# A first transform whose result is turned by DMA transposes in SBUF instead of a bounce through DRAM

## The chip, the cores and the metric

One core of one Trainium2 chip runs the kernel. The metric is the device time of one execution in microseconds (us); a kernel's time is the median of its runs. On one core a run counts as slow when it is over 1.5% above the fastest of the same kernel.

## The reference, cut to what matters

Two stages over x of 8 batches x 3072 tokens x 256 channels:

```python
X = np.fft.rfft(x, axis=1)                       # along the 3072 tokens
Yr = Xr @ w_r - Xi @ w_i + b_r                   # complex 256 x 256 product, soft shrink by 0.01
Yi = Xr @ w_i + Xi @ w_r + b_i
y = np.fft.irfft(Y, n=3072, axis=1)
# then, on y:
xk, xr = mu_k * y + (1 - mu_k) * y_prev, mu_r * y + (1 - mu_r) * y_prev
k = np.maximum(xk @ w_k, 0.0)                    # 256 -> 1024
out = sigmoid(xr @ w_r) * (k * k @ w_v)          # 1024 -> 256
```

## The kernel before: the parts that the change touches

The transform of 3072 = 96 x 32 points is made in two matmul stages. The first (96 points, matrix FT) is followed by a change of layout, the second (32 points, with twiddles, G) needs its rows by group. Then come the complex product (`mix`), the second transform's inverse (`back`, GI), a second change of layout through DRAM (Vdr, the "second bounce"), and the inverse of the first (`last`, FI). Tokens follow, six tiles of 512 per batch.

A Python scheduler with modelled durations decides the order in which each engine gets its instructions. `done[...]` holds the moment at which it assumes something to be there. The order is fixed when the program is built.

```python
    def first(b, t0, t1):                # batches 2 to 7: bounce through DRAM
        ...
                for i in range(2):
                    nc.tensor.matmul(ps[:96, 512 * i:512 * i + 512], FT,
                                     xt[:, 4 * p + 2 * i:4 * p + 2 * i + 2, :], start=True, stop=True)
        ...
                def store(k):
                    nc.sync.dma_start(out=Adr[b][:, 8 * q:8 * q + 8, :], in_=a)
        ...
                def fetch(k):
                    for hf in range(2):
                        A2[b, hf] = a2_pool.tile([128, NG // 2, D], BF16, name="A2")
                        for cj in range(4):
                            r0 = 24 * cj + 12 * hf
                            nc.sync.dma_start(out=A2[b, hf][32 * cj:32 * cj + 32],
                                              in_=Adr[b][r0:r0 + 12].rearrange("g n d -> n g d"))

    def direct(b, t0, t1, t2):           # batches 0 and 1: channels as rows, then turned on TensorE
        ...
                for i in range(8):
                    nc.tensor.matmul(pv[:, i, :], xt[:, i, 128 * c:128 * c + 128], FT, start=True, stop=True)
        ...
                    if c == 1 and b == 1:
                        load_x(2, q)     # x of batch 2
        ...
        def turn(u):                     # 8 identity matmuls and one copy out of PSUM, six times
        ...
    # in back(), after the last piece of V is in SBUF:
                def store(k):
                    for cj in range(4):
                        nc.sync.dma_start(out=Vdr[b][...], in_=vt[32 * cj:32 * cj + 32])
                    if u == NU - 1:
                        at(k + (3.0 if b == 0 else WRITE_US), fetch)      # WRITE_US = 5.0
                def fetch(k):
                    for q in (2, 3, 0, 1):
                        nc.sync.dma_start(out=V2[b, q], in_=Vdr[b][:, 8 * q:8 * q + 8, :])
                    done["V2", b] = k + READ_US                           # READ_US = 7.0
```

All of these DMAs, and the output stores, are issued by SP in one order (SP's lines below, from 198.89 us in the change, show it).

## Time and profile before

| | before |
|---|---|
| median, 4 runs beside the changed kernel | 617.68 us |
| span of the profiled run | 615.4 us |
| first W_k matmul (tokens begin) | 74.8 us |
| PE busy, mean granted clock | 571.8 us (93%), 0.987 |
| period of the steady part, start to start of one W_v group | 70.3 us, once 74.9 |

PE is TensorE, PEld its weight loads, DVE VectorE, ACT ScalarE, SP the engine that issues DMAs; "PE L609" is the matmul of line 609. The changed kernel's line numbers differ: W_k is L609 before and L560 after, W_v L653 and L604, the last transform L523 and L474, the second transform L381/L398 and L326/L343, the first transform in channels-as-rows form L335 and L279. In the versions made for the experiments the numbers shift again. The lines of the page and the trace stand in the prediction, with their readings. "The head" is the time until the tokens begin, "the steady part" the rest. In the lines, out<-in names what a transfer or an instruction writes and reads: Vdr<-V is a store of V, V<-Vdr its fetch, A<-X a transpose, xs<-in_x_dram a load of x. A line of a timeline begins with its start and its length in us. A "hole" is a time in which PE waits.

### The profile page before, as it was taken

The page shows a single profiled execution, that of the slowest core. Times are in us where ns is not written, and L with a number is a line of the kernel's source. Part 1 is how long each engine was busy: PE and PEld are TensorE (multiplying, and loading weights), DVE is VectorE, ACT ScalarE, POOL GpSimd, SP SyncE. Part 2 cuts the span into 40 slices and gives each one's busy share as a digit, 9 for nine tenths or more (in the row PEclk, how much of TensorE's full clock was granted, in tenths as well). Part 3 has the DMA queues.
Part 4 walks back from the last instruction along what each step waited for, and adds up shares of the span by engine and source line. Part 5 has one row for each costly group of instructions (what it writes and reads, how often), then busy time and mean ns, then how long its engine had stood idle before and what let it go on. Part 6 is the DMA issues. An engine that isn't in the chain of part 4 may idle for free.

```text
span 615.4 us, 12311 instructions
## 1 busy us (share of the span) xinstructions
PE 571.8 (93%) x4823; PEld 431.9 (70%) x4891; DVE 517.6 (84%) x839; ACT 436.0 (71%) x476; POOL 23.3 (4%) x52
## 2 busy tenths in 40 slices
PE   4775899999999999979999999999999999999995
PEld 3764666667777777657776778677776778777664
DVE  6774699878998999959988888979888889989883
ACT  6764596776877677757787768876787777667662
POOL 7001000000000000000000000000000000000000
PEclk9999799999999999989999999999999999999999
DMA  8948237982668755695568946686347833462223
GB/s 150 175 82 181 65 62 166 242 185 55 133 142 236 172 110 132 144 231 118 108 136 200 195 114 129 141 236 147 83 98 189 190 93 87 87 172 65 70 64 78
DMA packets 68686, 84.06 MB, mean 137 GB/s; under 512 B 8978, under 2 KB 53780, under 8 KB 68628
## 3 DMA queue, kind: packets, MB, share of 16 engines
q1 hardware_dynamic: 62916, 69.24, 45.4%
q0 software_dynamic: 5712, 14.03, 14.7%
q8 instruction: 38, 0.62, 0.4%
q14 instruction: 20, 0.16, 0.1%
HBM read 50.07 MB, written 47.19 MB: 158 GB/s over the span
## 4 chain that ended last, share of the span: by engine, by line
PE 79%; DMA 8%; DVE 5%; ACT 5%; issue 2%; SPq 1%; POOL 0%; ACTq 0%; POOLq 0%; DVEq 0%
PE banks L653 25%; PE banks L609 24%; PE banks L426 11%; PE banks L636 6%; DMA V<-Vdr 4%; DMA Vdr<-V 3%; PE banks L523 3%; PE banks L398 3%; PE banks L452 3%; PE banks L280 3%; ACT rl L615 2%; DMA xs<-in_x_dram 1%; DVE Y L442 1%; DVE z L440 1%; DVE V L229 1%
## 5 line engine op out<-in xcount | busy, mean ns | idle before, releaser
L615 ACT ACTIVATE rl<-banks 128x1024 bf16<-128x1024 f32 x192 | 195.4, 1033 | 76.1 <-PE banks L609 75.0
L609 PE MATMUL banks<-xk,wk 128*128 128x512 bf16 x700 | 190.1, 379 | 5.1 <-ACT A L227 0.8
L653 PE MATMUL banks<-wv,k 128*128 128x256 bf16 x1536 | 183.4, 273 | 0.3 <-DVE k L621 0.3
L653 PEld LDWEIGHTS <-k 128*128 128x128 bf16 x1536 | 149.6, 98 | 30.3 <-issue 1.2
L621 DVE TENSOR_TENSOR k<-rl 128x1024 bf16<-128x1024 bf16 x192 | 131.0, 685 | 16.8 <-ACT rl L615 16.1
L609 PEld LDWEIGHTS <-wk 128*128 128x128 bf16 x768 | 73.0, 97 | 59.5 <-issue 3.2
L426 PEld LDWEIGHTS <-XT 128*128 128x128 bf16 x768 | 74.4, 98 | 16.1 <-issue 0.6
L426 PE MATMUL banks<-wr,XT 128*128 128x256 bf16 x384 | 73.5, 273 | 0.2 <-ACT XT L227 0.2
L426 PE MATMUL banks<-wi,XT 128*128 128x256 bf16 x384 | 73.5, 273 | 0.0
L587 DVE SCALAR_TENSOR_TENSOR xk<-diff,muk,YT 128x512 bf16<-128x512 bf16 x96 | 70.0, 745 | 0.5
L587 DVE SCALAR_TENSOR_TENSOR xr<-diff,mur,YT 128x512 bf16<-128x512 bf16 x96 | 68.9, 745 | 0.0
L227 ACT ACTIVATE YT<-banks 128x768 bf16<-128x768 f32 x60 | 46.3, 814 | 30.0 <-PE banks L523 28.1
L660 DVE TENSOR_TENSOR o<-banks,rg 128x1024 f32<-128x1024 f32 x48 | 58.5, 1219 | 6.6 <-PE banks L653 6.6
L227 ACT ACTIVATE z<-banks 128x1024 bf16<-128x1024 f32 x39 | 39.9, 1024 | 23.7 <-PE banks L426 23.7
L227 ACT ACTIVATE XT<-banks 128x1024 bf16<-128x1024 f32 (+2 forms) x45 | 44.4, 989 | 14.3 <-PE banks L398 14.3
L636 PE MATMUL banks<-wrm,xr 128*128 128x256 bf16 x384 | 50.6, 275 | 1.8 <-ACT rl L615 1.7
L641 ACT ACTIVATE rg<-banks 128x1024 bf16<-128x1024 f32 x48 | 49.5, 1031 | 0.9 <-PE banks L636 0.9
L227 ACT ACTIVATE A<-banks 96x1024 bf16<-96x1024 f32 (+1 forms) x43 | 43.4, 1015 | 8.0 <-PE banks L280 6.7
L636 PEld LDWEIGHTS <-xr 128*128 128x128 bf16 x384 | 37.4, 98 | 12.7 <-issue 2.6
L523 PE MATMUL banks<-FI,V 96*128 96x96 f16 x512 | 33.5, 216 | 12.9 <-DMA V<-Vdr 12.6
L227 ACT ACTIVATE V<-banks 128x1024 bf16<-128x1024 f32 x35 | 36.0, 1028 | 13.2 <-PE banks L452 11.1
L523 PEld LDWEIGHTS <-V 96*128 96x128 bf16 x512 | 29.5, 104 | 20.6 <-DMA V<-Vdr 14.7
(98 smaller groups left out, 447.3 us busy)
## 6 DMA issues: line engine op xcount, KB each, us to landing
out_dram<-o SPq DMA_DIRECT2D x192, 128.0 KB, 2.3
xs<-in_x_dram POOLq DMA_DIRECT2D x32, 384.0 KB, 6.2
Vdr<-V SPq DMA_DIRECT2D x192, 64.0 KB, 1.8
V<-Vdr SPq DMA_DIRECT2D x32, 384.0 KB, 6.8
Adr<-A SPq DMA_DIRECT2D x24, 384.0 KB, 5.5
A<-Adr SPq DMA_DIRECT2D x48, 192.0 KB, 5.6
wk<-in_moe_w_k_dram POOLq DMA_DIRECT2D x1, 512.0 KB, 11.6
wv<-in_moe_w_v_dram POOLq DMA_DIRECT2D x1, 512.0 KB, 13.9
```

Of the source, the lines that this page charges most:

```text
L227: nc.scalar.activation(out, in_, AF.Copy, bias=0.0, scale=1.0)
L280: nc.tensor.matmul(ps[:96, 512 * i:512 * i + 512], FT, xt[:, 4 * p + 2 * i:4 * p + 2 * i + 2, :], start=True, stop=True)
L426: nc.tensor.matmul(o, lhs, w[:, c, :], start=(w is wr and c == 0), stop=(w is wi and c == NCD - 1))
L523: nc.tensor.matmul(pv[:, c, :, i, :], V2[b, n2 // 8][:, n2 % 8, 128 * c:128 * c + 128], FI, start=True, stop=True)
L587: nc.vector.scalar_tensor_tensor(out=m[:, c, :], in0=df[:, c, :], scalar=mu[:, c:c + 1], in1=yp[:, c, :], op0=ALU.mult, op1=ALU.add)
L609: nc.tensor.matmul(ps[:, 512 * f:512 * f + 512], wk[:, c, 128 * ff:128 * ff + 128], xk[:, c, :], start=(c == 0), stop=(c == NCD - 1))
L615: nc.scalar.activation(rl, ps, AF.Relu, bias=0.0, scale=1.0)
L621: nc.vector.tensor_tensor(out=k2, in0=rl, in1=rl, op=ALU.mult)
L636: nc.tensor.matmul(ps[:, 256 * q:256 * q + 256], xr[:, c, 128 * q:128 * q + 128], wrm[:, c, :], start=(c == 0), stop=(c == NCD - 1))
L641: nc.scalar.activation(rg, ps, AF.Sigmoid, bias=0.0, scale=1.0)
L653: nc.tensor.matmul(ps[:, 256 * q:256 * q + 256], K2[t][:, ff, 128 * q:128 * q + 128], wv[:, ff, :], start=(ff == 0), stop=(ff == NCF - 1))
L660: nc.vector.tensor_tensor(out=o.rearrange("p q d -> p (q d)"), in0=ps, in1=rg, op=ALU.mult)
```

## The change

Its intent: take the first bounce (3 MB through DRAM a batch) away from the DMA engines, make the first transform cheaper on TensorE, and free TensorE and the copy engines of the turning in batches 0 and 1. All batches now use the channels-as-rows form, and eight DMA transposes turn it inside SBUF. With it come a split of the two sine activations that make table G, the x loads of batch 2 moved behind the arrival of V of batch 0, a scheduler period of 70.5 instead of 71.5, and the last token tile in two parts.

```diff
+    PARTS = 4
     def first(b, t0, t1):
-        (16 matmuls 96x512 a batch, store to Adr by quarter, fetch by group)
+                for i in range(8):
+                    nc.tensor.matmul(pv[:, i, :], xt[:, i, 128 * c:128 * c + 128], FT, start=True, stop=True)
+                ...
+                def turn(k):
+                    n = NG // PARTS
+                    for i in range(PARTS):
+                        hf, g0 = n * i // 12, n * i % 12
+                        if g0 == 0:
+                            A2[b, hf] = a2_pool.tile([128, NG // 2, D], BF16, name="A2")
+                        for cc in range(NCD):
+                            nc.sync.dma_start_transpose(
+                                out=A2[b, hf][:, g0:g0 + n, 128 * cc:128 * cc + 128],
+                                in_=X1[b, cc][:, n * i:n * i + n].rearrange("p g r n -> p (g r n)"))
+                        for u in range(NU):
+                            if n * i < 4 * u + 4 <= n * i + n:
+                                done["A2", b, u] = k + 2.5 + 10.0 * (i + 1) / PARTS
-    def direct(b, t0, t1, t2):           (the PE turn of batches 0 and 1)
...
                     done["V2", b] = k + READ_US
+                    if b == 0:
+                        nc.gpsimd.tensor_copy(out=n1c[0:96], in_=V2[0, 1][:, 0, 0:1])
+                        for q in range(4):
+                            load_x(2, q)
...                                       (v_unit: the last tile in two halves, on the queues of SP and ACT)
-    P = 71.5
+    P = 70.5
```

The `tensor_copy` on GpSimd only makes that queue wait: it reads V2 and so holds the loads behind it. This hold is called "the gate" below.

More of the change, by code (lines that the diff above doesn't have):

```diff
@@ L55, in pool @@
         return ctx.enter_context(tc.tile_pool(name=name, bufs=bufs))
-    a_pool, a2_pool, xt_pool, xt0_pool = pool("ap", 3), pool("a2p", 4), pool("xtp", 3), pool("xt0p", 1)
+    x1_pool, a2_pool, xt_pool, xt0_pool = pool("x1p", 2), pool("a2p", 4), pool("xtp", 3), pool("xt0p", 1)
     r1_pool, ym_pool, v_pool, v2_pool = pool("r1p", 2), pool("ymp", 3), pool("vp", 3), pool("v2p", 4)
@@ L173, in make_g @@
     def make_g():
-        for j, sc in ((0, sc0), (1, sc1)):
-            nc.scalar.activation(G[:, :, :, j, :], ang, AF.Sin, bias=0.0, scale=sc)
+        nc.scalar.activation(G[:, :, :, 1, :], ang, AF.Sin, bias=0.0, scale=sc1)
         nc.vector.tensor_scalar(out=G0[:, 0], in0=G[:, 0, 1], scalar1=-1.0, scalar2=None, op0=ALU.mult)
@@ L262, in ready @@
             return None if f is None else max(r, f)
-    Adr, A2, Vdr, V2, YT = {}, {}, {}, {}, {}
+    X1, A2, Vdr, V2, YT = {}, {}, {}, {}, {}
     READ_US, WRITE_US = 7.0, 5.0
+    NU = NG // 4
+    PARTS = 4
     def first(b, t0, t1):
-        live = {}
-        def make(q, p):
-            def issue(ps, h, end):
-                if p == 0:
-                    if q == 0:
-                        Adr[b] = dram.tile([2 * 48, N2, D], BF16, name="Adr")
-                    live["A"] = a_pool.tile([96, 8, D], BF16, name="A")
-                xt, a = xs[b, q], live["A"]
-                for i in range(2):
-                    nc.tensor.matmul(ps[:96, 512 * i:512 * i + 512], FT,
-                                     xt[:, 4 * p + 2 * i:4 * p + 2 * i + 2, :], start=True, stop=True)
-                def evac(k):
-                    e = copy(k, a[:, 4 * p:4 * p + 4, :], ps[:96].rearrange("p (n d) -> p n d", n=4),
-                             1.03, 1.22)
-                    release(h, e)
-                    if p == 1:
-                        at(e, store)
-                def store(k):
-                    nc.sync.dma_start(out=Adr[b][:, 8 * q:8 * q + 8, :], in_=a)
-                    done["a", b, q] = k + WRITE_US
-                    n = 4 * b + q + 4
-                    if 8 <= n < 4 * B:
-                        load_x(n // 4, n % 4)
-                        done["x", n // 4, n % 4] = k + 9.0
-                    if q == 3:
-                        at(k + WRITE_US, fetch)
-                def fetch(k):
-                    for hf in range(2):
-                        A2[b, hf] = a2_pool.tile([128, NG // 2, D], BF16, name="A2")
-                        for cj in range(4):
-                            r0 = 24 * cj + 12 * hf
-                            nc.sync.dma_start(out=A2[b, hf][32 * cj:32 * cj + 32],
-                                              in_=Adr[b][r0:r0 + 12].rearrange("g n d -> n g d"))
-                        for u in range(3 * hf, 3 * hf + 3):
-                            done["A2", b, u] = k + READ_US * (1 + hf) / 2
-                at(end, evac)
-            needs = [("x", b, q), "FT"] + [("K", 0)] * (b == 2)
-            if q == 3 and p == 1 and b >= 2:
-                needs.append(("mid", b - 2))
-            if q == 0 and p == 0 and b >= 2:
-                needs.append(("A2", b - 2, NU - 1))
-            n = 4 * b + q - 3
-            if p == 0 and n >= 8:
-                needs.append(("a", n // 4, n % 4))
-            return Unit(t0 + (t1 - t0) * (2 * q + p) / 8, 0.44, needs, issue)
-        return [make(q, p) for q in range(4) for p in range(2)]
@@ L324, in direct @@
-    def direct(b, t0, t1, t2):
-        live = {}
         def make(q, c):
             def issue(ps, h, end):
-                if q == 0 and c == 0:
-                    live["X1"] = yt_pool.tile([128, NCD, NG, 4, 32], BF16, name="YT")
-                x1, xt = live["X1"], xs[b, q]
+                if q == 0:
+                    X1[b, c] = x1_pool.tile([128, NG, 4, 32], BF16, name="X1")
+                x1, xt = X1[b, c], xs[b, q]
                 pv = ps.rearrange("p (n f) -> p n f", n=8)[:, :, 0:96]
@@ L337, in evac @@
                 def evac(k):
-                    e = copy(k, x1[:, c, :, :, 8 * q:8 * q + 8], pv.rearrange("p n (r g) -> p g r n", r=4),
+                    e = copy(k, x1[:, :, :, 8 * q:8 * q + 8], pv.rearrange("p n (r g) -> p g r n", r=4),
                              0.82, 0.98)
@@ L341, in evac @@
                     done["x1", b, q, c] = e
-                    if c == 1 and b == 1:
-                        load_x(2, q)
-                        done["x", 2, q] = k + 9.0
-                at(end, evac)
-            return Unit(t0 + (t1 - t0) * (2 * q + c) / 8, 0.35, [("x", b, q), "FT"] + [("mid", 0)] * b, issue)
-        def turn(u):
-            def issue(ps, h, end):
-                if u % 3 == 0:
-                    A2[b, u // 3] = a2_pool.tile([128, NG // 2, D], BF16, name="A2")
-                for i in range(4):
-                    for c in range(NCD):
-                        nc.tensor.matmul(ps[:, 256 * i + 128 * c:256 * i + 128 * c + 128],
-                                         live["X1"][:, c, 4 * u + i].rearrange("p r n -> p (r n)"), ident,
-                                         start=True, stop=True)
-                def evac(k):
-                    e = copy(k, A2[b, u // 3][:, 4 * (u % 3):4 * (u % 3) + 4, :],
-                             ps.rearrange("p (g d) -> p g d", g=4), 1.03, 1.22)
-                    release(h, e)
-                    done["A2", b, u] = e
-                at(end, evac)
-            return Unit(t1 + (t2 - t1) * u / 6, 0.45, [("x1", b, 3, 0), ("x1", b, 3, 1)], issue)
@@ L370, in direct @@
-        return [make(q, c) for q in range(4) for c in range(2)] + [turn(u) for u in range(NU)]
-    NU = NG // 4
+                    m = 4 * b + q + 4
+                    if c == 1 and 12 <= m < 4 * B:
+                        load_x(m // 4, m % 4)
+                        done["x", m // 4, m % 4] = k + 9.0
+                    if c == 1 and q == 3:
+                        at(max(done["x1", b, 3, 0], e), turn)
+                def turn(k):
[11 more added lines that the diff above has]
+                                done["A2", b, u] = k + 2.5 + 10.0 * (i + 1) / PARTS
+                    done["tr", b] = k
@@ L374, in middle @@
+                at(end, evac)
+            needs = [("x", b, q), "FT"] + [("mid", 0)] * (b == 1) + [("K", 0)] * (b == 2)
+            if q == 0 and b >= 1:
+                needs.append(("tr", b - 1))
+            if q == 3 and c == 1 and b >= 2:
+                needs.append(("mid", b - 2))
+            return Unit(t0 + (t1 - t0) * (2 * q + c) / 8, 0.35, needs, issue)
+        return [make(q, c) for q in range(4) for c in range(NCD)]
     def middle(b, t0, t1):
@@ L477, in fetch @@
                     done["V2", b] = k + READ_US
+                    if b == 0:
+                        nc.gpsimd.tensor_copy(out=n1c[0:96], in_=V2[0, 1][:, 0, 0:1])
+                        for q in range(4):
+                            load_x(2, q)
+                            done["x", 2, q] = k + 12.0 + 4.0 * q
                 if u == NU - 1:
@@ L654, in issue @@
                                      wv[:, ff, :], start=(ff == 0), stop=(ff == NCF - 1))
-            if p == 0:
+            final = t == NT - 1
+            if p == 0 and not final:
                 return
-            o, rg = o_pool.tile([128, 4, D], FP32, name="o"), RG[t]
+            if p == 0 or not final:
+                OT[t] = o_pool.tile([128, 4 * D], FP32, name="o")
+            o, rg = OT[t], RG[t]
+            lo, hi = (512 * p, 512 * p + 512) if final else (0, 1024)
             def gated(k):
-                nc.vector.tensor_tensor(out=o.rearrange("p q d -> p (q d)"), in0=ps, in1=rg, op=ALU.mult)
-                e = run_on("dve", k, 1.22)
-                release(h, e)
+                nc.vector.tensor_tensor(out=o[:, lo:hi], in0=ps[:, lo:hi], in1=rg[:, lo:hi], op=ALU.mult)
+                e = run_on("dve", k, 0.7 if final else 1.22)
+                if p == 1:
+                    release(h, e)
                 at(e, store)
@@ L666, in store @@
                 b, half, hh = t // 6, (t % 6) // 3, t % 3
-                rows = out[b].rearrange("(h s z x q) d -> h z x s q d", h=3, s=32, z=2, x=4)
+                rows = out[b].rearrange("(h s z x q) d -> h z x s (q d)", h=3, s=32, z=2, x=4)
                 for xx in range(4):
-                    nc.sync.dma_start(out=rows[hh, half, xx], in_=o[32 * xx:32 * xx + 32])
+                    queue = nc.scalar if final and xx % 2 else nc.sync
+                    queue.dma_start(out=rows[hh, half, xx][:, lo:hi], in_=o[32 * xx:32 * xx + 32, lo:hi])
+            if p == 0:
+                at(end, gated)
+                return
             done["v_out", t] = end
@@ L724, in tables, with tables1 @@
     def tables(k):
+        nc.scalar.activation(G[:, :, :, 0, :], ang, AF.Sin, bias=0.0, scale=sc0)
+        at(run_on("act", k, 1.5) + 0.3, tables1)
+    def tables1(k):
         make_g()
-        run_on("act", k, 3.0)
-        done["G"] = run_on("dve", free["act"], 0.5)
-    P = 71.5
+        e = run_on("act", k, 1.5)
+        done["G"] = run_on("dve", e, 0.5)
+    P = 70.5
     START = 50.0
@@ L734 @@
         if b == 0:
-            fb += direct(b, 0.0, 1.0, 34.0)
+            fb += first(b, 0.0, 1.0)
             fa += middle(b, 17.0, 38.0)
@@ L738 @@
         elif b == 1:
-            fb += direct(b, 35.0, 36.0, 50.0)
+            fb += first(b, 35.0, 36.0)
             fa += middle(b, 37.0, 60.0)
```

## The prediction

> **What bounds the kernel now.** I read the page's busy line and slices first, then stretches of the run, then the chain of waits in the stretches with holes, then the two forms of the first transform.
>
> ```profile
> PE 571.8 (93%) x4823; PEld 431.9 (70%) x4891; DVE 517.6 (84%) x839; ACT 436.0 (71%) x476; POOL 23.3 (4%) x52
> ...
> PE   4775899999999999979999999999999999999995
> ```
>
> PE (TensorE) is full from about the sixth slice (15.4 us each) to the last but one; before that it has holes, and one nine turns to a seven in slice 18. The stretches (columns: window, its length, then busy us and instructions of PE, PEld, DVE, ACT, POOL, the granted clock, the DMA share, GB/s) size them:
>
> ```profile
> 18.00:30.00 12.00, 9.82 (x121) 8.75 (x119) 9.50 (x15) 8.21 (x9) 0.00 (x0) 1.00 1.04 180
> 45.00:57.00 12.00, 8.80 (x138) 7.53 (x135) 8.70 (x10) 8.84 (x11) 2.04 (x4) 1.00 0.93 174
> 57.00:66.00 9.00, 2.22 (x22) 1.59 (x23) 2.59 (x4) 0.17 (x1) 0.00 (x0) 0.68 0.66 175
> ...
> 155.00:195.00 40.00, 39.73 (x314) 29.66 (x317) 37.47 (x57) 29.98 (x33) 1.52 (x3) 1.00 0.75 173
> 263.00:273.00 10.00, 6.39 (x57) 4.38 (x56) 4.57 (x11) 4.68 (x6) 0.00 (x0) 0.83 0.82 243
> ```
>
> So the steady part is bound by PE's issue time. Its period is 70.3 us: the same pair of W_v matmuls starts at 354.01, 424.33 and 494.65 in the chain of waits. One period (208.83 to 283.69) takes 74.9: it loses 4.5 us. The head, until the first token tile begins at 74.7 us, is bound by latency. Its chain of waits:
>
> ```profile
> 13.53 3.00 ACT G L175 x2
> ...
> 44.82 1.03 ACT V L227
> ...
> 47.28 9.77 DMA Vdr<-V
> ...
> 58.57 6.67 DMA V<-Vdr
> ```
>
> These two transfers are the second bounce of batch 0, which the change keeps. A store of V takes a median of 1.8 us to land; here the last takes 9.8, because the x loads of batch 2 are released at 45.7 to 48.1 (four issues on POOL) and run beside it. While PE waits, its clock falls too: 0.68 is granted from 57 to 66.
>
> The first transform has two forms in this kernel. Batches 0 and 1 already use channels as rows (L335) and turn them on PE (L356); batches 2 to 7 use L280 and bounce through DRAM:
>
> ```profile
> 44.57 3.26 PE L335 MATMUL banks<-FT,xs 96*128 96x96 f16 x64
> 48.71 2.15 PE L356 MATMUL banks<-ident,YT 128*128 128x128 f16 x32 [0.88 <-ACT YT L227]
> ...
> 251.53 0.60 PE L280 MATMUL banks<-xs,FT 96*96 96x512 bf16 x2
> 251.97 1.03 PE L609 MATMUL banks<-xk,wk 128*128 128x512 bf16 x4
> ```
>
> The merged duration of a group is first start to last end and includes the last matmul's latency. What PE pays is start to start: two L280 cost 251.97 - 251.53 = 0.44 us, and 64 L335 cost (3.26 - 0.23) / 63 = 48 ns each.
>
> ```profile
> Adr<-A SPq DMA_DIRECT2D x24, 384.0 KB, 5.5
> A<-Adr SPq DMA_DIRECT2D x48, 192.0 KB, 5.6
> ```
>
> These rows are the removed bounce of batches 2 to 7. Nothing on PE waits for it by name: the waits of PE list only V<-Vdr (12.6 us in 8) among the DMAs after the head. It is hidden; it costs only DMA time.
>
> [...] L356 has a median duration of 219 ns and streams at about 60 ns. [...] No DMA transpose is in this trace. [...] The trace has 0.43 us for such an issue on SP. [...] 16 L335 of batch 0 take (1.46 - 0.235) / 15 = 82 ns each, those of batch 1 48, and 16 L523 of the same shape at 556.0 take 43.
>
> **Part 1, the first transform of batches 2 to 7 on PE.** Removed: 8 units of 0.44 = 3.5 us a batch. Added: 64 matmuls at 43 to 48 ns = 2.75 to 3.1 us. Gain 0.4 to 0.75, say 0.55 us a batch; six batches give **3.3 us**, all of it on PE's path, as the steady part is full. The copies out of PSUM become 8 of 0.81 (ACT) or 0.96 (DVE) instead of 8 of 1.02 or 1.22: 1.6 to 2.1 us of engine time less a batch, not on the path (ACT 30 and DVE 37.5 of 40 us).
>
> **Part 2, the turning.** Removed: 96 identity matmuls and their 12 copies (6.7 us busy on PE, 13.0 on ACT and DVE together), all in the head. Added everywhere: 8 DMA transposes a batch of 128x768 bf16, 192 KB each. [...] The change's own schedule assumes 2.5 + 10 us. I choose 10 to 13 us alone, up to twice that beside loads (both estimates). In the steady part they stand about 0.28 of a period, 20 us, ahead of their use, so they are hidden. They replace 3 MB of stores and loads a batch by 1.5 MB moved inside SBUF.
>
> **Part 3, the head.** For batch 0, the split of the two sine activations lets the last x copy go between them; the transposes can start near 16 us instead of the PE turn at 18.1. The first landing, about 4.5 us later under load (DMA share 1.04 from 18 to 30), comes near 20.5, where the second transform starts today. After that the transposes pace the middle stage (about 20 us for all beside the loads, so to 37), with its copies relieved of the turn's; the last V store lies between 42 and 47 instead of 46 to 47.7. Then the x loads of batch 2, moved behind V2's arrival, no longer lengthen its landing: 9.8 becomes about 4, which gives 5 to 6 us. Against it: batch 1's transposes now fall behind the fetch of V in SP's queue, so its middle stage has less done when the tokens start; I take 2 back, and add 1.5 for the earlier V stores. Head: **5 us** (0 to 9).
>
> **Part 4, the lost 4.5 us at 263 to 273.** There V<-Vdr took 8.2 us while the core moved 243 GB/s, among it Adr stores and x loads. With the first bounce gone and the order a little shifted I count half, **2 us**.
>
> **Part 5, the end.** After the last matmul today:
>
> ```profile
> 609.58 1.22 DVE L660 TENSOR_TENSOR o<-banks,rg 128x1024 f32<-128x1024 f32 x1 [3.16 <-PE banks L653]
> ```
>
> and the span ends at 615.4. In two parts the last product is half as long (about 0.65), two issues a queue instead of four save 0.86, and 64 KB land a little sooner than 128: **1.5 us**.
>
> Sum: 3.3 + 5 + 2 + 1.5 = 11.8. From 617.5 that is 605.7; I say **606**.
>
> **The rivals.** (a) The transposes are slow or hold SP: over 20 us a batch, 64 KB V stores and output stores wait behind them, the two output buffers run full (a token tile takes 7.8 us of PE, so a store may be late by at most about 15), and the steady part grows. [...] Against: the schedule's 10 us looks like a measured value, as its 7 and 5 us for reads and writes sit near the 6.8 and 5.5 of the page. It would make 620 to 680. (b) The V fetch falls behind batch 1's transposes in the head, or batch 0's pace is set by slow transposes; the head gains nothing or loses 3. For it: both are due within about a microsecond of each other in the schedule. Then 610 to 614. (c) Only PE's sum matters: 30 us more of L335 against 21 and 6 less is about even in busy time, so nothing moves. Against: busy time counts latency; by start-to-start it is 64 x 45 ns against 3.5 us. That rival gives 614. (d) Everything in the head comes through and the hole at 263 closes: 4.5 + 9 + 4 + 1.7, so about 598.
>
> **Range and chances.** The four terms have errors of about 1, 4, 2 and 0.5, together 4.7, plus the tail of (a): 8 in 10 between **598** and **614**. The 2% line is at 605.2, nearly my middle. Faster by over 2%: **0.47**; within 2%: **0.48**; slower by over 2%: **0.05**.
>
> **What would show it.** Part 1: start-to-start times of the periods near 69.7 instead of 70.3; above 70.3 it is wrong. Part 2: eight transposes landing within about 13 us of the first issue in the steady part, PE waiting for them nowhere there, and SP's gaps before output stores under 10 us. Part 3: last V store to V fetch under 6 us, first L609 at 67 to 71 instead of 74.7; if it stands above 74 the head failed. Part 4: no wait of PE for V<-Vdr over 1 us after the head. Part 5: last matmul to end of span near 4.3 us instead of 5.8. The whole is wrong if waits for A2 or for output buffers appear on PE or DVE in the steady part.

Where a cut is marked, statements stood that no trace or run shows. The "10 to 13 us alone, up to twice that beside loads" of part 2 and the "about 4.5 us later under load" of part 3 are estimates, beside the 2.5 + 10 us that the schedule assumes; no trace before the change had a transpose. The 0.43 us is for the issue of a plain DMA on SP (four fetches of V in 1.72 us, at 57.28). For "64 KB land a little sooner than 128" the DMA rows of the page before have 1.8 us (median) for the 64 KB stores of V and 2.3 for the 128 KB output stores.

## The result, and the profile after

The changed kernel takes 638.03 us (637.55 to 640.07, 4 runs) against 617.68 us (615.23 to 619.53): slower, ratio 1.034, 95% interval 1.030 to 1.038. A ratio here is the mean time of one kernel's fast runs over that of the other's in the same rounds, so not quite the ratio of the medians quoted. The prediction said 606, with 598 to 614.

The page after, its busy line and PE's slices (15.9 us each):

```profile
PE 568.3 (89%) x5014; PEld 435.1 (68%) x5083; DVE 510.9 (80%) x838; ACT 420.6 (66%) x466; POOL 23.4 (4%) x53
...
PE   4185588999999799989999799999999999999997
```

PE is busy for 3.5 us less in a span 20.6 us longer: the loss is waiting. The stretches of the head and one of the steady part, in the columns of the prediction:

```profile
18.00:30.00 12.00, 2.45 (x21) 1.90 (x18) 0.37 (x2) 2.85 (x3) 0.00 (x0) 1.00 1.30 164
...
57.00:66.00 9.00, 1.75 (x40) 1.60 (x36) 2.68 (x3) 2.58 (x4) 0.00 (x0) 0.85 0.72 181
66.00:75.00 9.00, 4.13 (x41) 3.52 (x42) 1.97 (x8) 2.92 (x4) 2.72 (x6) 0.58 1.11 196
...
195.00:235.00 40.00, 36.37 (x321) 26.92 (x325) 30.15 (x50) 24.54 (x28) 0.51 (x1) 0.96 0.71 146
```

From 18 to 30 us the compute engines do little: PE is busy for 2.45 of 12 us, where before it was for 9.8. What PE waited for over the run (sum, times, longest):

```profile
PE banks L326 <- DMA A<-X: 22.9, 4, 10.4
PE banks L474 <- DMA V<-Vdr: 11.7, 9, 3.1
...
PE banks L343 <- DMA A<-X: 4.3, 3, 2.5
```

A<-X are the transposes. All 27.2 us of these waits lie before 85 us; in the steady part only V<-Vdr is waited for. In the chain of waits the transposes stand twice in the head, and the fetch of V where the period is long:

```profile
16.45 16.16 DMA A<-X
...
71.13 13.39 DMA A<-X
...
202.13 9.78 DMA V<-Vdr
```

The ledger between the two traces: the first W_k matmul comes at 87.9 instead of 74.8 us (13.1 lost), and from there to the end it takes 548.1 instead of 540.6 us (7.5 lost). Together 20.6, the difference of the spans.

The DMA rows that answer to the removed bounce, and what became of the packets (before: 68686 packets, 8978 of them under 512 bytes):

```profile
DMA packets 98191, 77.78 MB, mean 122 GB/s; under 512 B 59090, under 2 KB 85460, under 8 KB 98132
...
q1 hardware_dynamic: 92228, 62.69, 45.6%
...
A<-X SPq DMA_TRANSPOSE x64, 4.2
```

The hardware queue moves 6.5 MB less than before (69.24) and takes the same share of the engines' time (45.4% before): the eight transposes of a batch move their 1.57 MB in 6144 packets of 256 bytes.

### The profile page after: what moved, and what is told of

The parts are those of the page before. It is cut to its first block, busy times and chain, and to the rows that moved or that the text cites. A ratio compares the mean times of both kernels' runs of the same rounds, so it can differ in the third digit from the quotient of the medians.

```text
span 636.0 us, 12660 instructions
## 1 busy us (share of the span) xinstructions
PE 568.3 (89%) x5014; PEld 435.1 (68%) x5083; DVE 510.9 (80%) x838; ACT 420.6 (66%) x466; POOL 23.4 (4%) x53
## 4 chain that ended last, share of the span: by engine, by line
PE 70%; DMA 14%; ACT 7%; DVE 3%; SPq 3%; issue 2%; POOL 0%; ACTq 0%; POOLq 0%; DVEq 0%
PE banks L604 24%; PE banks L560 21%; PE banks L371 11%; DMA V<-Vdr 7%; DMA A<-X 5%; PE banks L587 5%; PE banks L343 3%; PE banks L474 3%; ACT rl L566 3%; PE banks L397 2%; PE banks L279 2%; SPq L300 1%; DMA Vdr<-V 1%; DMA xs<-in_x_dram 1%; ACT V L226 1%
## 5 line engine op out<-in xcount | busy, mean ns | idle before, releaser
L604 PE MATMUL banks<-wv,k 128*128 128x256 bf16 x1536 | 187.2, 276 | 2.2 <-ACT rl L566 1.8
L604 PEld LDWEIGHTS <-k 128*128 128x128 bf16 x1536 | 151.7, 99 | 35.6 <-issue 5.1
L226 ACT ACTIVATE XT<-banks 128x1024 bf16<-128x1024 f32 (+2 forms) x40 | 39.5, 987 | 39.8 <-PE banks L343 29.1
L615 DVE TENSOR_TENSOR o<-banks,rg 128x1024 f32<-128x1024 f32 (+1 forms) x49 | 58.8, 1200 | 7.5 <-PE banks L604 7.5
L226 ACT ACTIVATE YT<-banks 128x768 bf16<-128x768 f32 x48 | 37.5, 813 | 26.8 <-PE banks L474 26.8
L226 ACT ACTIVATE V<-banks 128x1024 bf16<-128x1024 f32 x41 | 42.6, 1039 | 10.5 <-PE banks L397 9.6
L474 PE MATMUL banks<-FI,V 96*128 96x96 f16 x512 | 31.0, 212 | 11.9 <-DMA V<-Vdr 11.7
L533 DVE TENSOR_TENSOR diff<-YT 128x1024 bf16<-128x1024 bf16 x48 | 32.9, 685 | 10.3 <-ACT YT L226 10.2
L385 DVE TENSOR_TENSOR z<-z,bias 128x1024 bf16<-128x1024 bf16 x48 | 32.9, 685 | 7.0 <-ACT z L226 7.0
```

Of the source, the lines that this page charges most:

```text
L226: nc.scalar.activation(out, in_, AF.Copy, bias=0.0, scale=1.0)
L385: nc.vector.tensor_tensor(out=z, in0=z, in1=bias0 if u == 0 else bias, op=ALU.add)
L474: nc.tensor.matmul(pv[:, c, :, i, :], V2[b, n2 // 8][:, n2 % 8, 128 * c:128 * c + 128], FI, start=True, stop=True)
L604: nc.tensor.matmul(ps[:, 256 * q:256 * q + 256], K2[t][:, ff, 128 * q:128 * q + 128], wv[:, ff, :], start=(ff == 0), stop=(ff == NCF - 1))
L615: nc.vector.tensor_tensor(out=o[:, lo:hi], in0=ps[:, lo:hi], in1=rg[:, lo:hi], op=ALU.mult)
```

## The experiments

Sixteen versions ran, each correct, timed in three rounds beside the kernel before (617.3 to 618.7 us in the five sets). The sets ran on different chips; their times are compared as they stand, with about 1 us of play. In the table, "W_k" is the first W_k matmul in the profiled run, "rest" the time from there to the end of the span.

| run | transposes in batches | also changed | time, us | W_k | rest |
|---|---|---|---|---|---|
| before | none | | 617.7 | 74.8 | 540.6 |
| the change | 0 to 7 | | 638.0 | 87.9 | 548.1 |
| e1 | 2 to 7 | PE turn in 0, 1 | 615.1 | 66.0 | 547.4 |
| e1b | 1 to 7 | PE turn in 0 | 632.9 | 79.3 | 552.9 |
| e2 | 0, 1 | bounce in 2 to 7 | 624.3 | 85.9 | 533.8 |
| e3 | 0 to 7 | assumed landing | 635.5 | 74.0 | 559.2 |
| e4 | 0 to 7 | loads held for batch 0's | 632.5 | 81.5 | 551.6 |
| f4 | none | rest of the change kept | 602.3 | 66.9 | 533.9 |
| f1 | 2 to 7 | e1, last transform later | 619.0 | 67.3 | 549.9 |
| f2 | 2 to 7 | e1, transposes later | 613.9 | 66.1 | 546.8 |
| g1 | 2 to 7 | e1, transposes earlier | 654.4 | 67.2 | 582.5 |
| h1 | 2 to 7 | e1, V fetch earlier | 600.3 | 66.2 | 532.0 |
| k1 | 0 to 7 | V fetch earlier | 621.9 | 88.3 | 531.9 |
| k2 | 1 to 7 | e1b, x loads of batch 2 later | 625.5 | 73.9 | 551.4 |
| k3 | 0 to 7 | e4, k1 and k2's gate | 609.7 | 75.7 | 532.0 |
| m1 | none | f4, V fetch earlier | 603.6 | 66.5 | 535.1 |

The two remaining runs (g3, e6) are the kernel before with one part of the change each.

### Which half loses: the head or the steady part

**e1: PE turn in batches 0 and 1, transposes from batch 2 on.**

```diff
-                    if c == 1 and q == 3:
+                    if c == 1 and q == 3 and not (b < 2):
                         at(max(done["x1", b, 3, 0], e), turn)
...
+        def pe(u):      # as the PE turn of the kernel before: 8 identity matmuls, one copy, six units
```

> The changed kernel, but batches 0 and 1 turn their rows on TensorE with identity matmuls again (the x loads of batch 2 stay behind V2). Theory A (the loss is in the head: the transposes of batches 0 and 1 are slow and PE waits for A2 there): the waits of PE for A go away, the first W_k matmul comes at 68 to 73 us instead of 87.9, and the time is 616 to 622. Theory B (the transposes of batches 2 to 7 disturb the steady part): the first token tile is earlier too but the steady part keeps its three holes of 2.5 to 3.1 us before the last transform; under A alone they would be gone. Rival C (only the program order was unlucky in the steady part, the head is not the cause): 630 or more.

615.1 us, W_k at 66.0: A holds for the head, a little beyond its range there. 22.9 us of the 638.0 were the transposes of two batches. But B holds for the steady part: it stays long (547.4 us), with 3.1 to 3.9 us of holes at the last transform of each of batches 2, 3 and 4 (0.7 at 5 and 6). So A alone is not all, and the steady loss does not need the late head.

**e2: the other half.** The first transform of batches 2 to 7 is the old one with its bounce, batches 0 and 1 use transposes.

```diff
-            fb += first(b, s - 0.9 * P, s - 0.2 * P)
+            fb += bounced(b, s - 0.9 * P, s - 0.2 * P)   # the old first(), with Adr
```

> The other half: batches 0 and 1 by DMA transposes as in the change, batches 2 to 7 through the DRAM bounce of the kernel before. Theory A: the head stays as late as in the change (first W_k matmul 86 to 90 us) and the time is 627 to 634. If instead the steady transposes carry the loss (B), the time is 617 to 623.

624.3 us lies between the two ranges. The head is as late as in the change (85.9), the rest takes 533.8 us instead of 548.1. Both parts lose: about 23 us in the head by e1, about 14 us in the steady part by e2. That is more than the 20.6 us of the ledger because the other parts of the change gain, as the next run shows.

**f4: no transposes, all else of the change kept.** It is e1 and e2 together.

> No DMA transpose at all: PE turn in batches 0 and 1, DRAM bounce in 2 to 7, and all else of the change kept (x loads of batch 2 behind V2, split sine tables, period 70.5, last tile in two parts). If the transposes only cost and the rest of the change carries its gains: first W_k matmul at 66 to 67 us, steady part as with the bounce (533.7 us from there to the end), so 599 to 604. Rival (the steady part is without holes only by luck of order when the head is late): holes come back as in the kernel before, 605 to 611.

602.3 us, ratio 0.975 (0.971 to 0.979), W_k at 66.9 and no hole of more than 0.42 us after 81 us. The rest of the change is worth 15 us by itself; the transposes cost 36. Of these 15 us the gate gives 8.0 when it is alone (g3, below); the split of the sines and the new period were not run alone.

### The head: why the transposes came late

**e4: the loads of three quarters of x of batch 1 and of w_k, w_rm, w_v held until batch 0's transposes have landed.**

```diff
-        load_x(1, q)  ...  big["wk"] = load_w(...)  ...  (at the start)
+    load_x(1, 0)
...
                     done["tr", b] = k
+                    if b == 0:
+                        nc.gpsimd.tensor_copy(out=n1c, in_=A2[0, 1][:, 11, D - 1:D])
+                        (the held loads)
```

> The changed kernel with the loads of x of batch 1 (three of four) and of the weights w_k, w_rm, w_v held back until the last transpose of batch 0 has landed. Theory[...]: the first pair lands at 20 to 23 us instead of 28.9 to 32.6, all eight by 29 instead of 38, the last V store goes out 6 to 10 us earlier, and the time is 625 to 631. Rival (the transposes are as slow by themselves, from SP's 1.3 us of issue for each): the first lands no earlier than 28 and the time stays at 634 to 640.

The landings of the eight transposes of batch 0, from the trace of the change and of this run; the last line of each is minimum, median and maximum from issue to landing:

```profile
L300 SPq DMA_TRANSPOSE A<-X x8: 1286/1650/7769, 15.1 to 35.3; - x8
...
DMA to landing us min/median/max: 2.9/3.4/16.2
```

```profile
L300 SPq DMA_TRANSPOSE A<-X x8: 1271/1286/2041, 15.4 to 25.5; - x8
...
DMA to landing us min/median/max: 2.8/2.8/2.9
```

Undisturbed, a transpose of 192 KB lands 2.8 us after its issue and SP needs 1.29 us to issue each (0.43 for a plain DMA: four fetches of V in 1.72 us). The first lands at 18.2 and the last at 28.3, instead of 28.9 and 38.1: 1.57 MB in 12.9 us, 122 GB/s. In the trace's packet records of the change from 15 to 30 us, the software queue's loads sent 294 packets of 4096 bytes (349 ns each), 256 of 2048 and 999 of 512, while only 1268 of the 6144 packets of the transposes passed (55 ns each on average; 24 ns for the 6144 of batch 3, from 277 to 298 us). e4 takes the loads away whole: that they hold the transposes back is shown, by what mechanism is not. SP itself stood up to 7.8 us in one issue (9.1 among batch 1's), and its issues of eight transposes stretch over 11.4 us in e4 and 21.5 in the change (batch 0). The last V store went out at 50.8 instead of 58.2 us. The time, 632.5 us (628.4 to 636.2), misses the expected 625 to 631 by a little: PE then waits 9.0 us at one place for batch 1's transposes.

**e1b: PE turn in batch 0 alone.** The edit is e1's with `b < 1`.

> The changed kernel with batch 0 alone turned on PE, batch 1 and later by transposes. It splits the 21.9 us that the head transposes cost (87.9 against 66.0 us for the first W_k matmul, 638 against 615 us of time). If batch 0's slow start is the larger part: 620 to 625. If batch 1's (PE waits behind it for the last transform of batch 0): 626 to 633.

632.9 us. Batch 0's transposes cost 5.1 us (638.0 - 632.9), batch 1's 17.8 (632.9 - 615.1). Batch 1's lie behind the V fetch of batch 0 in SP's queue, and the x loads of batch 2, held until V is there, start beside them at 59.4 us: SP issued the eight from 52.2 to 74.8 us. Ahead of the last transform of batch 0 in PE's order stands the second transform of batch 1, which waits 10.3 us for the first pair.

**k2: those x loads held until batch 1's transposes have landed.**

```diff
-                    if b == 0:                                   (behind V2)
-                        nc.gpsimd.tensor_copy(out=n1c[0:96], in_=V2[0, 1][:, 0, 0:1])
+                    if b == 1:                                   (behind the transposes)
+                        nc.gpsimd.tensor_copy(out=n1c, in_=A2[1, 1][:, 11, D - 1:D])
                         for q in range(4):
                             load_x(2, q)
```

> The change with batch 0 turned on PE (632.9 us), the x loads of batch 2 held until the last transpose of batch 1 has landed instead of until V2 of batch 0 has. If those loads starve batch 1's transposes: all eight land within 16 us of the first issue instead of 23.4, first W_k matmul at 70 to 75 us instead of 79.3, 624 to 629. Rival (the fetch of V ahead of them in the same queue is what delays them): landing after 21 us or more, 631 to 635.

625.5 us, W_k at 73.9: SP had issued all eight by 65.8 instead of 74.8. So here too loads held the transposes back, all of 4096-byte packets this time (480 from 69 to 85 us in the change); that was 7.4 of the 17.8 us. But PE's wait of 10.3 us for the first pair is unchanged. That pair is issued behind the fetch of V and lands 7.3 us later (7.1 in e1b), as the x loads begin in e1b; for it the rival's mechanism, the fetch ahead of it, is the one left.

**e3: only the assumed landing corrected**, so that PE's order puts the last transform of batch 0 first.

```diff
-                                done["A2", b, u] = k + 2.5 + 10.0 * (i + 1) / PARTS
+                                done["A2", b, u] = k + {0: 17.5 + 2.0 * i, 1: 12.0 + 5.0 * i}.get(
+                                    b, 2.5 + 10.0 * (i + 1) / PARTS)
```

> The changed kernel with only the assumed landing of the transposes in its schedule corrected to what the trace showed for batches 0 and 1 (17.5 to 23.5 us and 12 to 27 us after the issue instead of 5 to 12.5); this moves no transfer, only the order in which PE gets its work: the last transform of batch 0 now stands ahead of the second transform of batch 1. If the order is what cost the head its second part: first W_k matmul at 76 to 82 us instead of 87.9, time 626 to 631. Rival (PE would only wait for the same transposes a little later): 633 to 638.

635.5 us: my theory falls and the rival holds. W_k came even earlier than expected, at 74.0, yet the gain was 2.5 us. The first output tile of batch 0 is multiplied by its sigmoid at 95.4 us instead of 110.5, but that of batch 1 at 166.2 instead of 169.6: PE waits 8.3 us for V of batch 0 instead of 15.0 for batch 1's transposes, and the middle stage of batch 1, put off, has to be done after the tokens have begun. The start of the tokens is no measure of the head by itself; what counts is how much work PE has got through.

### The steady part: three holes at the last transform

In the change, batch 2: SP's own line of issues, then PE. A number in brackets is the idle time before the instruction and what ended it.

```profile
198.89 1.73 SPq L626 DMA_DIRECT2D out_dram<-o  x4
200.79 1.76 SPq L421 DMA_DIRECT2D V<-Vdr  x4
202.65 15.69 SPq L300 DMA_TRANSPOSE A<-X  x8
...
211.95 1.02 PE L474 MATMUL banks<-FI,V 96*128 96x96 f16 x20 [2.52 <-DMA V<-Vdr]
213.91 3.34 PE L604 MATMUL banks<-wv,k 128*128 128x256 bf16 x16
```

SP issues an output store, then the fetch of V of batch 2, then the eight transposes of batch 3. The last `back` matmuls of the batch began at 192.5; the fetch goes out 8.3 us later, and PE's order has the last transform 15.2 us after `back`. In the kernel before those are 6.3 and 15.8 us in its quiet periods (batches 4 and 5: 6.3 and 6.6). After the hole the W_v group takes 3.34 us for 16 matmuls instead of 1.91: the clock has fallen (0.72 is granted from 212 to 218 us). Three candidates: the transposes right behind slow the fetch; the last transform comes too soon; the fetch goes out too late.

**f2: transposes issued 12 us later** in e1.

```diff
-                        at(max(done["x1", b, 3, 0], e), turn)
+                        at(max(done["x1", b, 3, 0], e) + 12.0, turn)
```

> The same kernel (615.1 us) with the transposes of batches 2 to 7 issued 12 us later by the schedule, so no longer right behind the fetch of V in SP's queue; the assumed landing of V stays at 7 us. If the transposes slow the fetch (E): last piece of V within 9 us of its issue instead of 11, the holes halve, 607 to 612. If only the place of the fetch and of the last transform counts (D): 612 to 617.

613.9 us, inside the range of D and outside that of E. Behind the fetch of batch 3 SP begins the transposes at 262.8 instead of 254.9 us, 10.0 us after the fetch instead of 1.8, and the hole there keeps 3.6 us (3.4 in e1). In batches 2 and 4 the last piece of V lands 10.3 and 10.5 us after the fetch (10.9 and 11.6 in e1), not within 9. All waits of PE for V come to 10.4 us instead of 12.4. So the transposes behind the fetch make at most a small part of the holes; the edit also moved some of PE's work.

**f1: the last transform later in PE's order** in e1.

```diff
-                    done["V2", b] = k + READ_US
+                    done["V2", b] = k + (READ_US if b == 0 else 11.0)
```

> The kernel with the PE turn in batches 0 and 1 and transposes in 2 to 7 (615.1 us), with one number of its schedule changed: from batch 1 on it assumes 11 us instead of 7 from the fetch of V to its landing, so PE gets more other work ahead of the last transform. Theory D (the steady holes are order: the fetch stands behind an output store in SP's queue and the last transform comes too soon after it): the holes of 2.6 to 3.9 us at the last transform fall under 1 us in all, the periods come to 69.5 to 70.3 us, the time to 601 to 607. Rival E (the transposes take the DMA engines whenever the fetch runs, so a later place only moves the wait): 611 to 616.

619.0 us: both ranges missed, the wrong way. What PE waited for from 100 to 600 us, in e1 and in f1:

```profile
PE banks L497 <- DMA V<-Vdr: 12.4, 10, 2.6
```

```profile
PE banks L349 <- DMA A<-X: 10.9, 9, 3.8
```

The wait for V is gone and one for the transposes has taken its place: with the last transform put off, PE reaches the next batch's second transform before the transposes have landed (batch 4's at 264.7 us; SP was issuing its transposes from 255.1). So the transposes have little to spare. In the change itself those of batch 3 are issued 21.9 us before PE's first use of them at 224.5, and the last lands at 219.9: 17.2 us after the first issue, 4.6 before that use.

**g1: the first transform 0.3 of a period earlier** in e1, to make that room.

```diff
-            fb += first(b, s - 0.9 * P, s - 0.2 * P)
+            fb += first(b, s - 1.2 * P, s - 0.5 * P)
```

> The kernel with the PE turn in batches 0 and 1 and transposes in 2 to 7 (615.1 us), the first transform of batches 2 to 7 due 0.3 of a period earlier, so that the transposes stand about 20 us ahead of the fetch of V instead of right behind it. If the steady loss is one of place (transposes and fetch due in the same 16 us, each needed within 15): no hole over 1 us in the steady part, 599 to 605, that is at least level with the version without transposes (602.3 us). Rival (transposes cost wherever they stand, as SP is held for over 10 us and V stores wait behind them): new holes at the back transform or the fetch, 608 to 618.

654.4 us, worse than either range. SP's line there:

```profile
164.58 6.57 SPq L433 DMA_DIRECT2D Vdr<-V  x7
171.25 12.50 SPq L300 DMA_TRANSPOSE A<-X  x8
183.85 1.97 SPq L433 DMA_DIRECT2D Vdr<-V  x4
...
195.19 1.72 SPq L444 DMA_DIRECT2D V<-Vdr  x4
```

The transposes now stand among the V stores and hold SP for 12.5 us, so the fetch goes out 18 us after `back` and PE waits 34.3 us in 14 places for V. The rival's mechanism is right, its size too small. In e1 and the change the place behind the fetch was the better one.

**h1: the fetch of V given to SP 2 us earlier** in e1, ahead of the output store. The assumed landing stays the same moment.

```diff
-                        at(k + (3.0 if b == 0 else WRITE_US), fetch)
+                        at(k + 3.0, fetch)
...
-                    done["V2", b] = k + READ_US
+                    done["V2", b] = k + (READ_US if b == 0 else 9.0)
```

> The same kernel (615.1 us) with the fetch of V given to SP 2 us earlier by the schedule in every batch, so it stands ahead of the output store; the assumed landing is the same moment. Theory: from the last back transform to the fetch 7 instead of 8.3 us, holes of 1.5 to 2.5 instead of 3.1 to 3.9 us, 608 to 613. Rival (the transposes right behind are what delays the pieces): 613 to 617.

600.3 us, ratio 0.974 (0.968 to 0.979), far better than expected. SP's line for batch 2:

```profile
173.04 2.72 SPq L433 DMA_DIRECT2D Vdr<-V  x4
177.37 1.72 SPq L444 DMA_DIRECT2D V<-Vdr  x4
179.14 1.94 SPq L649 DMA_DIRECT2D out_dram<-o  x4
181.24 14.74 SPq L300 DMA_TRANSPOSE A<-X  x8
```

The fetch goes out 6.8 us after `back`, and of the 12.4 us of waits for V in the steady part 0.6 are left. PE's order of work is the same in e1 and h1 from the first matmul to the last, so the place of the fetch in SP's queue is what counted: one output store ahead of it made holes of up to 3.9 us. A lower clock followed them: after the three long holes of the change 0.72, 0.55 and 0.72 was granted (212 to 218, 287 to 292.5 and 362 to 368 us). My expectation counted the two microseconds once. In fact the fetch goes out 1.4 us earlier, and its last piece lands 8.0 us after it (batch 3) instead of 10.9 and 11.6 (e1, batches 2 and 4); that is before PE reaches it, and the mean granted clock from 150 to 550 us is 1.00 instead of 0.99: from W_k to the end 532.0 instead of 547.4 us.

The traces show a partner of that store. In batches 2, 3 and 4 a load of x is issued 1.3 us after the fetch and runs beside it (180.1 to 189.9 us in e1). In batches 5 and 6 of e1 no x is left to load; the store stands ahead of the fetch and the fetch goes out 8.3 us after `back` as before, but the hole is 0.7 us. So the store made long holes only where a load ran too. In h1 that load is still there (180.2 to 188.7) and the holes are gone. No run moved these loads in the steady part.

**k1: the same edit in the whole change.**

> The whole change (638 us) with only the fetch of V given to SP 2 us earlier, as in the run that came to 600.3 us. If the steady loss is the place of the fetch and independent of the head: first W_k matmul still at 86 to 89 us, the three holes gone, 621 to 626. Rival (the cure works only with the early head): 630 or more.

621.9 us, W_k at 88.3, the rest 531.9 us, and no wait of PE over 0.45 us after 100 us. The steady cure does not need the early head.

**m1: the same edit where nothing is transposed (f4).**

> The version without any transpose (602.3 us) with the same earlier fetch, to hold against 600.3 us: if the cheaper first transform of the transposes carries 0.4 to 0.5 us a batch and nothing else differs, this one stays at 601.5 to 604. Rival (the earlier fetch helps the bounce as much): 599 to 601.

603.6 us, inside the range. With both layouts scheduled with this care, a steady period is 69.9 us with transposes (h1, k1: `last` of k1 begins at 278.0, 348.0, 417.9, 487.8) and 70.2 with the bounce (m1: 255.6, 325.9, 396.1). The transposes are worth about 0.3 us a batch; h1 against m1 is 600.3 against 603.6, with intervals of their ratios that meet (0.968 to 0.979, and 0.972 to 0.985), so the time itself doesn't resolve it.

### All three cures, and the parts that gain

**k3: transposes in all batches, with e4's held loads, k2's gate and k1's fetch.**

> Transposes in all batches with three cures: loads of x of batch 1 and of the weights held until batch 0's transposes have landed, x loads of batch 2 until batch 1's have, fetch of V 2 us earlier. If the three causes are all: 602 to 612, still above 600.3 by the later start of batch 1's middle. Rival (transposes in the head cost by their own 10 to 13 us, whatever runs beside): 613 to 622.

609.7 us, ratio 0.989. The three causes make up 28.3 of the 37.7 us between the change and h1. What is left, W_k at 75.7 instead of 66.2, is about PE's wait of 9.6 us for the first pair of batch 1, which stands behind the V fetch; in PE's fixed order nothing else comes first.

**g3: the kernel before with the x loads of batch 2 behind V alone** (the four lines of the change, and `load_x(2, q)` taken out of `direct`).

> The kernel before with one part of the change: the x loads of batch 2 wait for V2 of batch 0. The last V store of batch 0 lands within 4 us instead of 9.8, first W_k matmul at 67 to 70 us instead of 74.8, time 608 to 612. Rival (the head is set by other work): within 2 us of before.

609.3 against 617.3 us. The last V store of batch 0 lands in 2.8 us instead of 9.8 and W_k comes at 67.2.

**e6: the kernel before with the last tile in two parts alone.**

> The kernel before with the last token tile in two parts alone. Last matmul to end of span 4.2 us instead of 5.9, time 1.5 to 1.8 us less, nothing else moved.

From the last matmul to the end of the span 4.2 us (602.7 to 606.9), 5.9 before. The time does not resolve it: 616.1 against 617.3 us, ratio 0.997 (0.989 to 1.005). The runs of this kernel spread from 608.7 to 617.0, and those of the kernel before in that set from 611.4 to 618.8. The profiled run was the 608.7: its trace has no hole at 263 us, and its last V store of batch 0 lands in 5.2 us. So that hole does not come in every execution.

## Why the prediction was wrong

Its middle was 606 us; the change took 638. The terms, one by one:

- **Part 1** held in direction: units of 0.34 us instead of 0.44 (a unit of eight starts at 198.30 us in the change, the next matmul at 198.64). The sum was 0.55 us a batch; measured between h1 and m1 it is about 0.3.
- **Part 2 is the step that failed**, at its last words: "In the steady part they stand about 0.28 of a period, 20 us, ahead of their use, so they are hidden." The sizes were right: issued 21.9 us ahead of their use, 12.9 us long alone (e4; predicted 10 to 13), 17.2 beside other traffic (up to twice that), and in the steady part of the change PE never waits for them. What failed is that a hidden transfer was taken to cost nothing. In the new order an output store goes out ahead of the fetch of V, the fetch comes 2 us later after `back` than before (8.3 instead of 6.3), and PE waits for V at the last transform, 3.1 to 3.4 us in each of batches 2, 3 and 4. h1 and k1 put the fetch ahead of that store and take back 15 and 16 us without touching the transposes or PE's order.
- The second failure is in **part 3**: "The first landing, about 4.5 us later under load" took 13.8 us, and PE needed the second half of the pair too, 32.6 us. The size "about 20 us for all beside the loads, so to 37" was right (38.1). I had spread the delay evenly over the eight; it fell on the first, and everything waited for that. By e1b this cost 5.1 us. And "I take 2 back" for batch 1's transposes was 17.8 us. Part 3 had their place behind the fetch of V right, but not that PE stands still until their first pair lands (10.3 us), nor that the gate on the x loads, which it counted as a gain, releases these loads exactly beside them (7.4 us in k2).
- The gain that part 3 gave to the gate is real: 8.0 us in g3, against 5 to 6.
- **Part 4**: instead of losing a hole, the change got three, again by a late fetch of V. In the kernel before, the fetch of batch 3 went out 10.4 us after `back`, for another reason, which part 4 had not read: the V store took 7 us to land. One reading beside it was off, without weight in the sum: of the 12.6 us of waits for V "after the head", 8.7 lie in the head (61.4 to 65.3 us) and 3.9 after it.
- **Part 5** held: 1.7 us against 1.5.

Of its rivals, (a) had the mechanism of the steady part (SP's in-order queue: the fetch 8.3 us after `back` behind an output store, 6.8 in h1 ahead of it) and a range, 620 to 680, that holds the result, but it looked for the loss at output buffers, where no wait appeared, and it was given little chance (0.05 for slower). A sum of parts missed that the parts share one queue. e1 and h1 find 37.7 us lost to the transposes, 22.9 in the head and 14.8 at the fetch; k3 wins 28.3 of them back by queue order and the time of loads alone. Without the transposes the change gains 15 us (f4), where the prediction had 11.8 for all of it.

Open: whether a place exists in SP's order where the transposes are both early enough and out of the way (g1 and f2 tried two). How much of each long hole the x load made that ran beside the fetch. And why the six periods gained 0.3 us each and not the 0.7 by which their eight first-transform units shrank (a median of 0.342 us each instead of 0.435).

## What to carry to other kernels

When a transfer is replaced, look at what stands before and behind it in its issuing queue, not only at how long it takes: here one store ahead of the critical fetch of each batch cost 15 us, and moving the fetch two microseconds in the schedule won it back. Here bulk loads delayed a first landing from 2.8 to 13.8 us, so keep them away from the time of a transfer that something waits for, and check that a gate which helps one transfer doesn't release its loads upon the next (7.4 us here, by k2). And before giving a bundle of changes up, take it apart: without its title part this one is 602 us, with that part only where it has room and an earlier fetch 600 us, which the runs don't tell apart, against 618.
